# Half-tile products 2 and 4 for a second token group, with their weight sums formed by GpSimd

## The chip, the cores and the metric

One core of one Trainium2 chip runs the whole program. The metric is device time in microseconds (us), taken as the median of several executions; one further execution is recorded by the hardware profiler, and the views below come from it.

## What is computed

Sigmoid attention over 8 batches and 12 heads, then a two-layer network with squared ReLU over the 3584 tokens, all in fp32:

```
scores = q @ k.T / sqrt(64) - log(448)         # 8 x 12 heads, 448 x 448
x = sigmoid(scores) @ v                         # -> 3584 tokens x 768
h = x @ w_in                                    # 768 -> 2048
out = square(maximum(h, 0)) @ w_out             # 2048 -> 768
```

## The kernel before

Every fp32 operand is held as two words, high and low, and every product is three passes of matmuls (high x high, high x low, low x high). The two layers of the network are matrix products in the Strassen-Winograd form: seven products of half-size blocks, numbered 1 to 7, in place of eight. The tokens lie in four groups, g = 0 to 3; each half of a group holds 512 tokens (256 in the last). A group has two stages: the first (`gemm1`, m = 0) multiplies x by w_in, the second (`gemm2`, m = 1) multiplies the squared result by w_out. A step of the first stage is (n, i): product n, block i of the eight blocks of 128 rows of half of the hidden width. It is nine matmuls of 512 columns, three chunks of the depth by three passes.

`STEPS` says in what order a stage's steps come, `sequence` strings the stages together. `run_steps` walks over it and at each step issues what `stream` has put there for later steps: the load of a unit of weights LOAD_AHEAD = 9 steps before its use, and its split into two words HALVE_AHEAD = 5 steps before (ScalarE makes the high word, VectorE the low one; `halve`, L391 and L393). A unit of first-stage weights is up to two products of one block, 128 x 768 numbers: products 1 and 2 together, then 6 and 7, then 3 and 5, and 4 alone. The order of instructions on each engine is then left to a scheduler, except on TensorE in the stage of group `PAIRED`.

In that stage (group 2 before) two blocks are worked on together, and products 2 and 4 have a *halved* form: a second level of the same scheme on the first two chunks of two blocks, seven products of 128 x 256 (`seven`, L440), and the third chunk in the plain form (L678). The halved form needs four sums of 128 x 128 pieces of the weights of each block pair. Before, these are made during group 1's first stage by `prepare`: SyncE (SP) loads the pieces, VectorE adds and splits them, SP stores them; group 2 loads them back (`fetch_sums`).

PSUM has eight banks in four pools of two. `bank` gives the next pool by a counter, `turn`, modulo three, unless a pool is named; the fourth (number 3) is only given by name. After a product that starts or ends a sum, ScalarE copies the bank out (`snap`, L859, or `put`, L1108 with a store by ScalarE at L1109). Before, the first two steps of group 1's first stage are products 1 and 2 of block 0, in banks named ha and hc; oa are the output banks of a second stage.

## Time and profile before

| | us |
|---|---|
| median of 3 runs | 1049.09 (1049.04 to 1049.69) |
| the profiled execution | 1049.4 |
| its span in the trace | 1047.4 |
| group 1, first stage (474.26 to 588.50) | 114.24 |
| group 2, first stage (700.58 to 813.38) | 112.80 |

The span is what the profiler saw, from the first to the last instruction; the rest of an execution lies around it. A stage's length is the distance between the first matmuls of two stages. A row of a timeline gives the start, the duration, the engine, the line, the operation with output and inputs and their shapes, and in brackets for how long the engine was idle before and what ended that.

### The profile page before, as it was taken

How to read it: one execution, taken by the hardware profiler on the slowest of the kernel's cores; microseconds unless marked ns; L12 is line 12 of the kernel's file. 1: busy time of each engine (PE TensorE's matmuls, PEld its weight loads, DVE VectorE, ACT ScalarE, POOL GpSimd, SP SyncE). 2: the span in 40 equal slices, each digit the busy share in tenths (PEclk: the TensorE clock that was granted, in tenths of full speed). 3: DMA queues.
4: the chain of work that ended last, by engine and by line, in shares of the span. 5: the costliest groups of instructions: out<-in, count | busy, mean ns of one | idle time of the engine just before them, and what ended most of it. 6: DMA issues, size and time to landing. Idle time of an engine off the chain costs nothing.

```text
span 1047.4 us, 17472 instructions
## 1 busy us (share of the span) xinstructions
PE 1043.4 (100%) x6490; PEld 820.6 (78%) x6490; DVE 881.1 (84%) x1227; ACT 693.3 (66%) x974; POOL 124.9 (12%) x100
## 2 busy tenths in 40 slices
PE   9999999999999999999999999999999999999998
PEld 4555555557888888888888888888888888899987
DVE  5999999877778899696776799989777999957997
ACT  7989888877667856446444667555435757647973
POOL 1322231200222256300000000110000000000000
PEclk9999999999999999999999999999999999999999
DMA  9999999993567677985574968984445878955662
GB/s 357 400 370 384 343 401 364 329 335 115 185 206 243 213 257 262 335 310 186 169 234 129 320 219 289 323 285 150 139 133 190 273 254 312 316 182 184 182 204 97
DMA packets 127445, 266.45 MB, mean 254 GB/s; under 512 B 12160, under 2 KB 66176, under 8 KB 127360
## 3 DMA queue, kind: packets, MB, share of 16 engines
q1 hardware_dynamic: 125920, 262.91, 73.5%
q10 hardware_dynamic: 1440, 2.43, 0.6%
q8 instruction: 51, 0.84, 0.3%
q14 instruction: 34, 0.28, 0.1%
HBM read 199.75 MB, written 65.54 MB: 253 GB/s over the span
## 4 chain that ended last, share of the span: by engine, by line
PE 100%; DVE 0%; issue 0%
PE ha L678 22%; PE oa L678 19%; PE pav L365 11%; PE sc L334 9%; PE hb L678 8%; PE oq L440 6%; PE ob L678 5%; PE hc L678 3%; PE oc L678 3%; PE oa L686 2%; PE hq L440 2%; PE sr L350 2%; PE pav L377 2%; PE hb L686 1%; PE ob L686 1%; PE oa L689 1%
## 5 line engine op out<-in xcount | busy, mean ns | idle before, releaser
L393 DVE TENSOR_TENSOR w<-w 128x768 fp32r<-128x768 f32 (+1 forms) x159 | 146.7, 931 | 44.0 <-ACT w L391 32.9
L391 ACT CAST w<-w 128x768 fp32r<-128x768 f32 (+1 forms) x160 | 124.2, 795 | 44.9 <-DMA w<-w 42.9
L322 ACT ACTIVATE at<-sc 128x896 f32<-128x896 f32 x144 | 119.3, 943 | 3.9 <-PE sc L334 3.9
L365 PE MATMUL pav<-at,v 64*64 64x448 f32 x1152 | 118.1, 540 | 0.0
L365 PEld LDWEIGHTS pav<-at,v 64*64 64x64 f32 x1152 | 41.6, 133 | 60.8 <-issue 53.6
L786 ACT CAST w<-w 128x768 fp32r<-128x768 f32 x56 | 46.7, 836 | 39.4 <-DMA w<-w 34.5
L859 ACT COPY s<-ha 128x512 f32<-128x512 f32 (+1 forms) x48 | 24.8, 516 | 71.4 <-PE ha L678 65.2
L224 POOL TENSOR_TENSOR a<-a,f 128x768 int32<-128x768 int32 x24 | 52.8, 2202 | 159.5 <-DVE a L221 94.1
L644 DVE TENSOR_TENSOR ql<-x,qh 128x896 fp32r<-128x896 f32 x46 | 67.9, 1518 | 0.0
L334 PE MATMUL sc<-qh 64*128 64x448 f32 x282 | 53.9, 379 | 0.0
L334 PE MATMUL sc<-ql,qh 64*128 64x448 f32 x282 | 51.3, 360 | 0.0
L334 PE MATMUL sc<-qh,ql 64*128 64x448 f32 x282 | 50.9, 358 | 0.0
L387 DVE TENSOR_TENSOR xo<-pav,xo 128x448 f32<-128x448 f32 x48 | 29.5, 621 | 24.4 <-ACT xo L383 22.6
L678 PE MATMUL oa<-o_0h,w 128*128 128x512 f32 x144 | 46.3, 389 | 0.0
L678 PE MATMUL oa<-o_1h,w 128*128 128x512 f32 x144 | 46.3, 389 | 0.0
L678 PE MATMUL oa<-o_2h,w 128*128 128x512 f32 x144 | 46.3, 389 | 0.0
L678 PE MATMUL oa<-o_3h,w 128*128 128x512 f32 x144 | 46.3, 389 | 0.0
L678 PE MATMUL ha<-x_0h,w 128*128 128x512 f32 x128 | 44.7, 390 | 0.0
L678 PE MATMUL ha<-x_2h,w 128*128 128x512 f32 x128 | 44.6, 389 | 0.0
L678 PE MATMUL ha<-x_1h,w 128*128 128x512 f32 x128 | 44.6, 389 | 0.0
L334 PEld LDWEIGHTS sc<-qh 64*128 64x128 f32 x282 | 26.4, 184 | 18.5 <-PE pav L365 16.2
L383 ACT COPY xo<-pav 128x448 f32<-128x448 f32 x48 | 25.5, 532 | 22.6 <-PE pav L377 10.9
(660 smaller groups left out, 3045.7 us busy)
## 6 DMA issues: line engine op xcount, KB each, us to landing
w<-w SPq DMA_DIRECT2D x195, 384.0 KB, 3.7
w<-h SPq DMA_DIRECT2D x56, 384.0 KB, 4.8
x<-qk SPq DMA_DIRECT2D x47, 448.0 KB, 6.8
f<-w_in SPq DMA_DIRECT2D x16, 768.0 KB, 9.0
v<-v SPq DMA_DIRECT2D x24, 448.0 KB, 6.8
xd<-xo SPq DMA_DIRECT2D x48, 224.0 KB, 5.4
h<-w SPq DMA_DIRECT2D x28, 384.0 KB, 4.1
w<-s SPq DMA_DIRECT2D x48, 192.0 KB, 7.5
```

Of the source, the lines that this page charges most:

```text
L224: nc.gpsimd.tensor_tensor(out=wb, in0=wb, in1=t.bitcast(I32)[:, :, 0], op=ALU.add)
L322: nc.scalar.activation(at, sc, AF.Sigmoid, bias=NEG_LOG_S, scale=SCALE)
L334: nc.tensor.matmul(sc[:, j], x[kp][rows, 1, ks], x[qp][rows, 0], start=(n == 0), stop=(n == len(passes) - 1),)
L365: nc.tensor.matmul(sums[columns, h], vt[rows, n % 2 * NT + t, columns], at[t][rows, j], start=(t == 0 and (n % 2, h) != (1, 1)), stop=(t = ...
L387: nc.vector.tensor_add(out=x, in0=sums[:, 0], in1=x)
L391: nc.scalar.copy(out=hi, in_=raw)
L393: nc.vector.tensor_sub(out=lo, in0=raw, in1=hi.bitcast(F32))
L440: nc.tensor.matmul(out, a, b, start=opens and c == 0 and half == 0, stop=closes and c == 2, skip_group_check=True)
L644: nc.vector.tensor_sub(out=xs[n][1], in0=x[n], in1=xs[n][0].bitcast(F32))
L678: nc.tensor.matmul(out, a[:, c], b, start=first and n == 0, stop=last and n == 2, skip_group_check=True)
L686: nc.tensor.matmul(out, w[0][:, c], x, start=first, stop=False, skip_group_check=True)
L786: nc.scalar.copy(out=hi, in_=hi.bitcast(F32))
```

## The change

- `PAIRED` becomes (1, 2): group 1's first stage has the form that group 2's has, products 2 and 4 halved, in the same order of steps, with TensorE's order fixed.
- In groups 1 and 2 a unit of first-stage weights is one product of two blocks (128 x 2 x 384 numbers, runs of 1536 bytes) where it was two products of one block (runs of 3072 bytes).
- `prepare` goes. In group 1 the sums are formed from the unit already loaded: GpSimd adds (`add_sums`, five steps ahead of the use), ScalarE and VectorE split (`split_sums`, three steps ahead), SP stores them for group 2 (`keep_sums`, at the use). Group 2 fetches them as before.
- The differences of x that the halved form needs are made for group 1 too, on GpSimd (`differ`), and group 1's operands of x follow the table `PAIRED_X`.

```
@@ -67,10 +67,8 @@
 LEAD = [(1, 0), (2, 0), (1, 1), (2, 1), (6, 0), (7, 0), (6, 1)]
 LEAD += [(5, 0), (7, 1), (3, 0), (1, 2), (2, 2), (4, 0)]
 
-CROSS = LEAD[:-4] + [(4, 0), (3, 0), (1, 2), (2, 2)]
 STEPS = LEAD + [s for s in ROUNDS if s not in LEAD] + TAIL, ROUNDS + TAIL
-STEPS += (CROSS + [s for s in ROUNDS if s not in LEAD] + TAIL,)
-PAIRED, HALVES_IN = 2, (2, 4)
+PAIRED, HALVES_IN = (1, 2), (2, 4)
 STEPS += ([(n, i + e) for i in range(0, NI, 2) for n in (1, 6, 2, 7, 5, 4, 3) for e in range(2)],)
 
 BEHIND = {512: [(7, Y), (5, Y), (4, Y), (3, Y)], 256: [(7, Z), (4, Y)]}
...
@@ -497,7 +494,7 @@
                 split_to(hi, lo, t, later)
 
         def differ(product, name):
-            if g == PAIRED:
+            if g in PAIRED:
                 raw["d", product] = flat2(f"xd{product}_{g}")
                 flat = raw[name][0].rearrange("p k s -> p (k s)")
                 differences(flat, raw["d", product], lambda **t: nc.gpsimd.tensor_tensor(op=ALU.subtract, **t))
@@ -691,16 +688,14 @@
 
     def order_of(g, m):
         if m == 0:
-            return STEPS[(0, 2, 3, 1)[g]]
+            return STEPS[(0, 2, 2, 1)[g]]
         return ORDERS if g < NG - 1 else [*ORDERS[:-NI], LAST]
 
     sequence = [(g, m, n, i) for g in range(NG) for m in range(2) for n, i in order_of(g, m)]
 
     def units_of(g, m, n, i):
-        if m == 0 and g == PAIRED:
-            if n == 4:
-                return [(g, m, i - i % 2, SPOT[n][0])]
-            return [(g, m, j, SPOT[n][0]) for j in ((i, i + 1) if n == 2 and i % 2 == 0 else (i,))]
+        if m == 0 and g in PAIRED:
+            return [(g, m, i - i % 2, n)]
         if m == 0:
             return [(g, m, i, SPOT[n][0])]
         return [(g, m, j, n) for j in (range(NI // 2) if i < 0 else (i // 2,))]
@@ -715,8 +710,8 @@
     def fetch(unit):
         g, m, i, u = unit
         both = m == 1 and g in TWICE_IN
-        if m == 0 and g == PAIRED and u == SPOT[4][0]:
-            src = w1[i : i + 2, :, UNITS[u].start].rearrange("i p c -> p i c")
+        if m == 0 and g in PAIRED:
+            src = w1[i : i + 2, :, PLACE[0][u]].rearrange("i p c -> p i c")
         elif m == 0:
             src = w1[i][:, UNITS[u]]
         else:
@@ -729,56 +724,58 @@
                     nc.sync.dma_start(out=t.bitcast(F32), in_=s2[i, TWICE.index(u), :, c])
             else:
                 raw_sums[unit] = op1(f"s{m}_{g}_{i}_{u}", WIDE)
-                weight_sums(loaded[unit][1].bitcast(F32), raw_sums[unit])
+                raw = loaded[unit][1].bitcast(F32)
+                weight_sums([raw[:, k, e * P : e * P + P] for e in range(2) for k in range(2)], raw_sums[unit])
 
     summed, raw_sums, front = {}, {}, {}
 
-    def weight_sums(raw, to):
-
-        a11, a12, a21, a22 = (raw[:, k, e * P : e * P + P] for e in range(2) for k in range(2))
+    def weight_sums(parts, to):
+
+        a11, a12, a21, a22 = parts
         s1, s2, s3, s4 = (to[:, n * P : n * P + P] for n in range(4))
         nc.gpsimd.tensor_tensor(out=s1, in0=a21, in1=a22, op=ALU.add)
         nc.gpsimd.tensor_tensor(out=s2, in0=s1, in1=a11, op=ALU.subtract)
         nc.gpsimd.tensor_tensor(out=s3, in0=a11, in1=a21, op=ALU.subtract)
         nc.gpsimd.tensor_tensor(out=s4, in0=a12, in1=s2, op=ALU.subtract)
 
-    halves, half_sums = {}, {}
-
-    def prepare(i, n):
-
-        def load():
-            halves[i, n] = t = flat2(f"sa{n}_{i}")
-            src = w1[i : i + 2, :, PLACE[0][n], : 2 * P].rearrange("i p c -> p i c")
-            nc.sync.dma_start(out=t[:, :WIDE].rearrange("p (i c) -> p i c", i=2), in_=src)
-
-        def add_up():
-            t = halves[i, n]
-            a11, a12, a21, a22 = (t[:, k * P : k * P + P] for k in range(4))
-            s_1, s_2, s_3, s_4 = (t[:, k * P : k * P + P] for k in range(4, 8))
-            nc.vector.tensor_add(out=s_1, in0=a21, in1=a22)
-            nc.vector.tensor_sub(out=s_2, in0=s_1, in1=a11)
-            nc.vector.tensor_sub(out=s_3, in0=a11, in1=a21)
-            nc.vector.tensor_sub(out=s_4, in0=a12, in1=s_2)
-            halves[i, n] = both = flat2(f"sh{n}_{i}", F32R)
-            split_to(both[:, :WIDE], both[:, WIDE:], t[:, WIDE:])
-
-        def store():
-            to = s1[i // 2, HALVES_IN.index(n)]
-            nc.sync.dma_start(out=to, in_=halves.pop((i, n)).bitcast(F32))
-
-        return load, add_up, store
+    half_sums, raw_halves = {}, {}
+
+    def half_sum_tiles(unit):
+        g, m, i, n = unit
+        half_sums[unit] = tuple(op1(f"sf{n}_{g}_{i}{c}", WIDE, F32R) for c in "hl")
+        return half_sums[unit]
+
+    def add_sums(unit):
+        g, m, i, n = unit
+        raw = loaded[unit][1].bitcast(F32)
+        t = raw_halves[unit] = flat2(f"sa{n}_{i}")[:, :WIDE]
+        weight_sums([raw[:, e, k * P : k * P + P] for e in range(2) for k in range(2)], t)
+
+    def split_sums(unit):
+        split_to(*half_sum_tiles(unit), raw_halves.pop(unit))
+
+    def kept_sums(unit):
+        g, m, i, n = unit
+        return s1[i // 2, HALVES_IN.index(n)].rearrange("p (c s) -> c p s", s=WIDE)
+
+    def keep_sums(unit):
+        for to, t in zip(kept_sums(unit), half_sums[unit]):
+            nc.sync.dma_start(out=to, in_=t.bitcast(F32))
 
     def fetch_sums(unit):
-        i, n = unit
-        half_sums[unit] = tuple(op1(f"sf{n}_{i}{c}", WIDE, F32R) for c in "hl")
-        for c, t in enumerate(half_sums[unit]):
-            src = s1[i // 2, HALVES_IN.index(n)][:, c * WIDE : c * WIDE + WIDE]
+        for t, src in zip(half_sum_tiles(unit), kept_sums(unit)):
             nc.sync.dma_start(out=t.bitcast(F32), in_=src)
 
-    for i in range(0, NI, 2):
-        for n in HALVES_IN:
-            use = sequence.index((PAIRED, 0, n, i))
-            stream.setdefault(use - HALF_SUMS_AHEAD[n], []).append((fetch_sums, (i, n)))
+    for unit in units:
+        g, m, i, n = unit
+        if m == 0 and g in PAIRED and n in HALVES_IN:
+            use = first_use[unit]
+            if g == PAIRED[0]:
+                pieces_at = (HALVE_AHEAD, add_sums), (SUMS_SPLIT, split_sums), (-SUMS_KEPT, keep_sums)
+            else:
+                pieces_at = ((HALF_SUMS_AHEAD[n], fetch_sums),)
+            for ahead, piece in pieces_at:
+                stream.setdefault(use - ahead, []).append((piece, unit))
 
     def halve(unit, later=None):
         if unit[1] == 1 and unit[0] in TWICE_IN:
...
@@ -865,16 +862,16 @@
                 nc.vector.tensor_add(out=t, in0=both[:, n_tok:], in1=t)
 
         def weights_at(n, i):
+            if g in PAIRED:
+                return tuple(t[:, i % 2] for t in loaded[g, 0, i - i % 2, n])
             u, at = SPOT[n]
-            if n == 4:
-                i, at = i - i % 2, i % 2
             return tuple(t[:, at] for t in loaded[g, 0, i, u])
 
         def halved(n, i):
 
             for at in range(4):
                 banks["q", at] = bank(f"hq{n}_{g}_{i}_{at}", WIDE, 2 + at // 2)
-            w, s = [weights_at(n, i + e) for e in range(2)], half_sums.pop((i, n))
+            w, s = [weights_at(n, i + e) for e in range(2)], half_sums[g, 0, i, n]
 
             def part(k, h):
                 return tuple(t[:, h * Q : h * Q + Q] for t in ops[n][k])
...
@@ -926,17 +923,16 @@
         def run(n, i):
             count = len(pending)
             k = CHAIN[n]
-            if g == PAIRED and n in HALVES_IN:
+            if g in PAIRED and n in HALVES_IN:
                 run_halves(n, i)
                 return
-            if g == PAIRED and n in (1, 7):
+            if g in PAIRED and n in (1, 7):
                 banks[k, i] = bank(f"h{k}_{g}_{i}", n_tok, (1, 7).index(n))
             elif n in (1, 7, 2):
                 banks[k, i] = bank(f"h{k}_{g}_{i}", WIDE if n in BESIDE else n_tok, 3 if k == "c" else None)
             out = banks[k, i]
             beside = n_tok < WIDE and n in BESIDE
-            u, at = SPOT[n]
-            w = tuple(t[:, at].rearrange("p (c m) -> p c m", m=P) for t in loaded[g, 0, i, u])
+            w = tuple(t.rearrange("p (c m) -> p c m", m=P) for t in weights_at(n, i))
             parts = [(out, w, c, ops[n][c], n in (1, 7, 2) and c == 0, c == NE - 1) for c in range(NE)]
             if beside:
                 side_by_side(parts)
@@ -975,7 +971,7 @@
             run(n, i)
             if (n, i) in behind:
                 operand(behind[n, i])
-            if g == PAIRED and (n, i) == STEPS[3][-1]:
+            if g in PAIRED and (n, i) == STEPS[2][-1]:
                 while next(turn) % 3 < 2:
                     pass
 
@@ -1210,7 +1206,7 @@
                 for name in LATE_X.get((n, i), ()) if g == NG - 2 else ():
                     next_x[g][name]()
             if m == 0 and 0 < g < NG - 1:
-                for name in (PAIRED_X if g == PAIRED else EARLY_X).get(at - sequence.index((g, 0, *order_of(g, 0)[0])), ()):
+                for name in PAIRED_X.get(at - sequence.index((g, 0, *order_of(g, 0)[0])), ()):
                     next_x[g - 1][name]()
 
     made, second, next_x, postponed, now = {}, {}, {}, {}, [0]
@@ -1265,17 +1261,14 @@
         for n, piece in work:
             between.setdefault(n, []).append(piece)
         run_steps(0, len(STEPS[0]), between)
-    between = {}
-    begin = sequence.index((PAIRED - 1, 0, *order_of(PAIRED - 1, 0)[0])) + PREPARE_FROM
-    for n, (i, k) in enumerate((i, k) for i in range(0, NI, 2) for k in HALVES_IN):
-        load_piece, add_piece, store_piece = prepare(i, k)
-        for ahead, piece in ((0, load_piece), (4, add_piece), (6, store_piece)):
-            between.setdefault(begin + n * PREPARE_EVERY + ahead, []).append(piece)
-    first, second_stage = (sequence.index((PAIRED, m, *order_of(PAIRED, m)[0])) for m in range(2))
-    run_steps(len(STEPS[0]), first, between)
-    with tc.manual_schedule(engines={mybir.EngineType.PE}):
-        run_steps(first, second_stage, between)
-    run_steps(second_stage, len(sequence), between)
+    begin = len(STEPS[0])
+    for g in PAIRED:
+        first, second_stage = (sequence.index((g, m, *order_of(g, m)[0])) for m in range(2))
+        run_steps(begin, first, {})
+        with tc.manual_schedule(engines={mybir.EngineType.PE}):
+            run_steps(first, second_stage, {})
+        begin = second_stage
+    run_steps(begin, len(sequence), {})
 
 
 def kernel(q, k, v, moe_w_in, moe_w_out):
```

What moves on the engines is shown at three places. The first is TensorE at the start of group 1's first stage, with the semaphores that a row waits for; ha_1_0 and ha_1_1 are the banks of product 1, blocks 0 and 1, of group 1. Before:

```order
L678 MATMUL ha_1_0_5282<-y1_1l_5038,w0_1_0_0_5178 128x512
L678 MATMUL ha_1_0_5282<-y1_1h_5037,w0_1_0_0_5178 128x512
L678 MATMUL hc_1_0_5304<-x2_1h_5076,w0_1_0_0_5178 128x512
L678 MATMUL hc_1_0_5304<-x2_1l_5077,w0_1_0_0_5178 128x512
L678 MATMUL hc_1_0_5304<-x2_1h_5076,w0_1_0_0_5178 128x512 x2
```

And there TensorE has now:

```order
L675 MATMUL ha_1_0_5294<-y1_1l_5038,w0_1_0_1_5183 128x512
L675 MATMUL ha_1_0_5294<-y1_1h_5037,w0_1_0_1_5183 128x512
L675 MATMUL ha_1_1_5310<-x1_1h_5035,w0_1_0_1_5183 128x512 [waits Activation_49]
L675 MATMUL ha_1_1_5310<-x1_1l_5036,w0_1_0_1_5183 128x512
L675 MATMUL ha_1_1_5310<-x1_1h_5035,w0_1_0_1_5183 128x512 x2
```

Product 2 of block 0, in the fourth pool, stood second; now product 1 of block 1 does, and its first matmul waits for ScalarE, for the copy of the bank's last content, oa_0_2.

The second place is ScalarE there: w0_... are units of weights, o12_0_0 to o12_0_2 the copies of group 0's last output blocks, sf2_1_0h the high words of the first set of sums. Before:

```order
L391 CAST w0_1_0_1_5226<-w0_1_0_1_5226 128x768
L1108 COPY o12_0_0_5260<-oa_0_0_4289 128x512
L1109 DMA outT<-o12_0_0_5260 128x512
L1108 COPY o12_0_1_5274<-oa_0_1_4290 128x512
L1109 DMA outT<-o12_0_1_5274 128x512
L1108 COPY o12_0_2_5277<-oa_0_2_4291 128x512
L1109 DMA outT<-o12_0_2_5277 128x512
L859 COPY s1_1_0_5292<-ha_1_0_5282 128x512
L391 CAST y7_1h_5298<-yx11_1_4939 128x512
```

And ScalarE now:

```order
L388 CAST w0_1_0_2_5231<-w0_1_0_2_5231 128x768
L1104 COPY o12_0_0_5265<-oa_0_0_4289 128x512
L1105 DMA outT<-o12_0_0_5265 128x512
L1104 COPY o12_0_1_5277<-oa_0_1_4290 128x512
L1105 DMA outT<-o12_0_1_5277 128x512
L1104 COPY o12_0_2_5280<-oa_0_2_4291 128x512
L388 CAST sf2_1_0h_5321<-sa2_0_5283 128x512
L1105 DMA outT<-o12_0_2_5280 128x512
L388 CAST y7_1h_5331<-yx11_1_4939 128x512
L856 COPY g11_1_0_5304<-ha_1_0_5294 128x512
```

The copies keep their order behind the cast of a weight unit; the cast of the sums and that of y7 now stand ahead of the copy of product 1, block 0.

The third place is GpSimd from the last sums of group 0's second stage on: xd2_1 and xd4_1 are differences of x of group 1, sa2_0 and sa4_0 the sums for products 2 and 4 of the first block pair. Before:

```order
L743 TENSOR_TENSOR s1_0_3_4_4959<-w1_0_3_4_4957,s1_0_3_4_4959 128x128
L503 TENSOR_TENSOR xd2_2_7113<-x21_2_6946 128x256 x2
L503 TENSOR_TENSOR xd2_2_7113<-x21_2_6946,xd2_2_7113 128x256 x2
L503 TENSOR_TENSOR xd4_2_7379<-x21_2_6946 128x256 x2
L503 TENSOR_TENSOR xd4_2_7379<-x21_2_6946,xd4_2_7379 128x256 x2
```

And GpSimd now:

```order
L739 TENSOR_TENSOR s1_0_3_4_4959<-w1_0_3_4_4957,s1_0_3_4_4959 128x128
L500 TENSOR_TENSOR xd2_1_5097<-x21_1_4942 128x256 x2
L500 TENSOR_TENSOR xd2_1_5097<-x21_1_4942,xd2_1_5097 128x256 x2
L736 TENSOR_TENSOR sa2_0_5283<-w0_1_0_2_5231 128x128
L738 TENSOR_TENSOR sa2_0_5283<-w0_1_0_2_5231 128x128
L737 TENSOR_TENSOR sa2_0_5283<-sa2_0_5283,w0_1_0_2_5231 128x128
L739 TENSOR_TENSOR sa2_0_5283<-w0_1_0_2_5231,sa2_0_5283 128x128
L500 TENSOR_TENSOR xd4_1_5350<-x21_1_4942 128x256 x2
```

Where GpSimd had nothing between group 0's second stage and group 2's operands, it now makes the differences of group 1 and eight sets of four sums.

## Rows read from the trace of the kernel before

**Rows 1.** The page: busy time with shares and instructions; shares of the ending chain.
```profile
PE 1043.4 (100%) x6490; PEld 820.6 (78%) x6490; DVE 881.1 (84%) x1227; ACT 693.3 (66%) x974; POOL 124.9 (12%) x100
...
PE 100%; DVE 0%; issue 0%
```

**Rows 2.** Table by stretches, one stage each: length, busy time by engine, clock, DMA.
```profile
core 0: us, PE busy (x) PEld busy (x) DVE busy (x) ACT busy (x) POOL busy (x), PEclk, DMA share, GB/s
364.14:474.26 110.12, 110.12 (x488) 91.18 (x486) 98.38 (x101) 62.20 (x81) 43.25 (x48) 1.00 0.86 296
474.26:588.50 114.24, 114.24 (x506) 94.59 (x504) 78.09 (x119) 55.98 (x88) 0.00 (x0) 1.00 0.59 191
588.50:700.58 112.08, 112.08 (x614) 97.78 (x612) 104.36 (x145) 70.20 (x87) 6.50 (x6) 1.00 0.83 283
700.58:813.38 112.80, 112.80 (x578) 96.71 (x576) 89.73 (x123) 57.60 (x86) 1.64 (x3) 1.00 0.51 162
```

**Rows 3.** TensorE's timeline: first matmuls of steps in group 1, then group 2.
```profile
474.26 0.39 PE L678 MATMUL ha<-x_1h,w 128*128 128x512 f32 x1
...
476.30 0.39 PE L678 MATMUL hc<-x_1h,w 128*128 128x512 f32 x1
...
708.74 0.28 PE L440 MATMUL hq<-x_2h,w 128*128 128x256 f32 x1
...
712.64 0.39 PE L678 MATMUL hb<-x_2h,w 128*128 128x512 f32 x1
```

**Rows 4.** ScalarE's timeline just ahead of group 2's first stage.
```profile
698.06 0.59 ACT L1108 COPY o<-oa 128x512 f32<-128x512 f32 x1 [5.32 <-PE oa L678]
```

**Rows 5.** ScalarE's timeline at the start of group 1's first stage; ACTq is its queue.
```profile
473.67 0.84 ACT L391 CAST w<-w 128x768 fp32r<-128x768 f32 x1 [1.32 <-DMA w<-w]
474.40 0.58 ACT L1108 COPY o<-oa 128x512 f32<-128x512 f32 x1
475.02 2.74 ACTq L1109 DMA_DIRECT2D outT<-o  x1
477.80 0.59 ACT L1108 COPY o<-oa 128x512 f32<-128x512 f32 x1 [2.81 <-issue]
...
478.82 0.59 ACT L1108 COPY o<-oa 128x512 f32<-128x512 f32 x1 [0.44 <-PE hc L678]
...
479.87 0.59 ACT L859 COPY s<-ha 128x512 f32<-128x512 f32 x1 [0.47 <-ACT o L1108]
480.35 0.62 ACT L391 CAST y_1h<-yx 128x512 fp32r<-128x512 f32 x1
```

**Rows 6.** L1109 alone, ScalarE's stores: duration ns least/median/most, first and last start.
```profile
L1109 ACTq DMA_DIRECT2D outT<-o x9: 338/339/2737, 475.0 to 926.3; - x9
```

**Rows 7.** GpSimd's groups by line and shape: sums of weights (busy, mean ns, idle before).
```profile
L742 POOL TENSOR_TENSOR s<-w 128x128 f32<-128x128 f32 x12 | 12.5, 1042 | 0.0
L741 POOL TENSOR_TENSOR s<-s,w 128x128 f32<-128x128 f32 x12 | 12.3, 1023 | 0.1
L740 POOL TENSOR_TENSOR s<-w 128x128 f32<-128x128 f32 x12 | 10.7, 896 | 48.6 <-DMA w<-w 48.6
L743 POOL TENSOR_TENSOR s<-w,s 128x128 f32<-128x128 f32 x12 | 9.0, 750 | 0.5
```

**Rows 8.** VectorE's groups by line and shape: low words of `prepare`'s sums.
```profile
L393 DVE TENSOR_TENSOR sh<-sa,sh 128x512 fp32r<-128x512 f32 x8 | 5.5, 686 | 0.8 <-ACT sh L391 0.7
```

**Rows 9.** VectorE's timeline: one operation beside GpSimd's sums, one without.
```profile
373.18 1.20 DVE L393 TENSOR_TENSOR w<-w 128x768 fp32r<-128x768 f32 x1 [0.90 <-POOL s L743]
...
472.41 0.95 DVE L393 TENSOR_TENSOR w<-w 128x768 fp32r<-128x768 f32 x1
```

**Rows 10.** L296, landing of weight loads: 364 to 460 us, then 479 to 560.
```profile
DMA to landing us min/median/max: 3.2/4.3/8.5
...
DMA to landing us min/median/max: 2.3/3.3/4.6
```

**Rows 11.** SP's timeline ahead of group 1's first stage: its third unit.
```profile
468.73 0.37 SPq L296 DMA_DIRECT2D w<-w  x1
```

11 lines of the change are left out of this document (5 added, 6 removed).

## The prediction

> **What bounds the kernel now.** I read the shares of busy time and the chain of work first. TensorE is busy for 1043.4 of 1047.4 us and the chain that ended last is 100% TensorE [rows 1], so the time changes only by what TensorE has to do and by the pauses that it gets. Then the table by stretches, one row a stage. Group 1's first stage, the one that the change rewrites, is 474.26 to 588.50: 114.24 us, TensorE busy for all of it. Group 2's, 700.58 to 813.38, already has the form that group 1 is to get: 112.80 us, TensorE again never idle [rows 2]. The other engines have room in both: VectorE 78.09 and 89.73 us, ScalarE 55.98 and 57.60, GpSimd 0 and 1.64, and the granted clock is 1.00, the 2.4 GHz level [rows 2]. Last, TensorE's and ScalarE's timelines where the stage begins, since that is where the instructions move most.
>
> The profiled execution took 1049.4 us: its span of 1047.4 and 2.0 around it. The median of the runs is 1049.1, that is 0.3 less. I add up against 1049.4 and take the 0.3 off at the end.
>
> **What the change can give.** A step of nine 512-column matmuls takes 476.30 - 474.26 = 2.04 us, a pair of steps 4.08. In group 2 a halved pair goes from 708.74 to 712.64: 3.90 us [rows 3]. Each halved pair saves 0.18; products 2 and 4 have four pairs each, so 8 x 0.18 = 1.44 us. The stages say the same: 114.24 - 112.80 = 1.44 [rows 2]. **Term 1: -1.44 us.** As TensorE never idles in the stage today there is nothing else to win: 1.44 us, 0.14% of the time, is the ceiling. A measurement of this kernel can tell about 0.2% (2.1 us) from no change, so a full success would read as no change. What decides is whether TensorE now pauses somewhere.
>
> **The pause that the order adds.** Group 0's last product, 3, leaves three output blocks oa in three PSUM banks. ScalarE copies them out (L1108) and issues a store after each (L1109). In the order of before the second step of group 1's stage is product 2, whose bank hc is of the fourth pool and waits for nothing. In the order of after the second step is product 1, block 1, and its first matmul waits for ScalarE. The bank it is given is that of oa_0_2, the *third* copy: the paired form fixes product 1 to pool 0, and group 0's stages leave the counter `turn` where oa's blocks 0, 1, 2 lie in pools 1, 2, 0. Group 2 has the same step and does not suffer, since after a paired stage the counter is set so that block 0 lies in pool 0: only the first copy stands ahead of it, at 698.06, almost 2 us before the stage begins [rows 4, 2].
>
> ScalarE at that place in before: the cast of a weight unit at 473.67, the first copy at 474.40, a store whose issue takes 2.74 us, the second copy at 477.80, the third at 478.82 for 0.59, so to 479.41 [rows 5]. That store is the first of nine that ScalarE issues; the median of the nine is 0.339 us and the largest 2.737 [rows 6]. The order of after has the same sequence (weight cast, copy, store, copy, store, copy) and again this is the first transfer that ScalarE issues, so I take the long issue to come back, in the same place. TensorE reaches the step at 476.30 [rows 3] and the bank is free at 479.41: **term 2: 479.41 - 476.30 = +3.11 us.** Bounds: without the long issue the copies follow 1.02 us apart (478.82 - 477.80), the third from 474.40 + 2 x 1.02 = 476.44 to 477.03, and the wait is 0.73. Below nothing it cannot go, since TensorE waits for nothing at this place today. The row at this very place has the long issue; I take 3.11.
>
> What TensorE does next is product 6, block 0, into the bank of product 1, block 0, which must have been copied. Behind the third copy ScalarE now has the cast of the new sums, a store, a cast of y7 and that copy: 479.41 + 0.62 + 0.34 + 0.62 + 0.59 = 481.58 by [rows 5, 6], and casts overlap by some 0.1 there. TensorE ends product 1 at 479.41 + 2.04 = 481.45. **Term 3: 0** (bounds 0 and +0.2; when the third copy is early, up to +0.5, since the cast waits for GpSimd's sums).
>
> **The sums on GpSimd.** A set of four 128x128 operations takes 0.896 + 1.042 + 1.023 + 0.750 = 3.71 us [rows 7], eight sets 29.7 us, in a stage of 113 where GpSimd has nothing else but the eight operations for the differences. A set is begun five steps (10 us) ahead of its use and split after two. It hides behind TensorE; if a set came late, the halved product would wait for it. VectorE loses the adds of the sums and keeps their second words: 8 x 0.686 = 5.5 us [rows 8], on group 2's 89.73: 95.2. Beside GpSimd one VectorE operation on 128x768 took 1.20 us where it takes 0.95 alone [rows 9]; a quarter us for some 32 operations is 8 us, an estimate, and makes 103 of 112.8. Group 1's second stage runs at 104.36 of 112.08 without a pause, and in group 0's second stage GpSimd made such sums (43.25 us) beside 98.38 us of VectorE, TensorE still busy for all of 110.12 [rows 2]. **Term 4: 0**, up to +1 if a late set meets a bank.
>
> This is where a rule speaks against the change. In [rows 9] GpSimd lengthens an operation of VectorE by 0.25 us. The Trainium skill, page "SBUF — State Buffer", section "Who interferes with whom", says that GpSimd has no ports of its own but VectorE's second pair, and that this pair is an exclusive lock. By the rows the stage costs VectorE 103 us and nothing of the time; by the rule taken in full, 125 us, the rival below.
>
> **Weight loads.** The units of groups 1 and 2 become one product of two blocks: as many bytes, in runs of 1536 bytes where they were 3072. The second stages read such runs: loads landed in 3.2, 4.3 and 8.5 us (least, median, most) in group 0's second stage; in group 1's first stage with the long runs in 2.3, 3.3 and 4.6 [rows 10]. The DMA share is 0.86 in the one stretch and 0.59 in the other [rows 2], so the runs are not the whole difference. Loads are asked for nine steps, 18 us, ahead; 8.5 is covered, **term 5: 0**. The one place with less cover is the start of the stage, where the third unit was asked for at 468.73 and its cast began at 473.67, 4.94 us later [rows 11, 5]. That cast stands ahead of the three copies on ScalarE, in both orders. **Other edits** at no price: the early loads and VectorE adds of `prepare` go (2 MB less to read), the stores of the sums move to the steps that use them, behind operands long made; the operands of x come by the table that group 2 has, where they were in time.
>
> **Sum.** -1.44 + 3.11 + 0 + 0 + 0 = +1.67: 1049.4 + 1.67 = 1051.07 for the profiled run, less 0.3: **1050.8 us**.
>
> **The rivals.**
> *Short issue.* The store's issue takes 0.34 us, or the copies come before it. Wait 0.73, then up to 0.5 for the copy of product 1: -1.44 + 1.23 = -0.2, 1048.9. For it: eight of nine issues are short, and nothing that the long one waited for was open. Against: the long one is the first, and the first stays the first.
> *The gain in full.* The scheduler's order runs so that the copies are out by 476.3: 1047.65. Against: TensorE's last matmul into oa_0_2 ends about where the stage begins, and three copies with two stores are over 2 us of ScalarE.
> *A later landing (slower).* The third unit is now product 2 of two blocks, 256 short runs. If it lands later than the 4.94 us of before, its cast holds the three copies and the bank one for one. 8.5 us, the longest landing [rows 10], would add 3.6; I take +1.5, so 1052.3. It decides from a delay of 0.4 us. For it: the DMA engines are busiest there. Against: the median, 4.3, is below 4.94.
> *The clock falls.* TensorE has not paused at any place of before, and the granted clock was 1.00 in every row [rows 2]. If a pause of 3 us drops it to the 1.2 GHz level, each step of 2.04 us takes 4.08 until it rises; one to two steps cost 2 to 4, I take 3: 1053.8. The Trainium skill, page "TensorE: Matmul & The Clock Gate", section "HAM oscillation — how this bites in real kernels", tells of a clock lost in waits between bursts of matmuls; no row of this trace shows it.
> *VectorE becomes the bound.* If every us of GpSimd stops VectorE, the stage takes 95.2 + 29.7 = 124.9 us where it took 114.24: 10.7 more, 1059.8. Against: group 0's second stage, where 98.38 + 43.25 fitted into 110.12 [rows 2]. The rule on the ports named above would have it so.
> That the change does not do what it says is ruled out by the order: the halved steps and the sums stand where they should.
>
> **How the numbers follow.** Forecast 0.49 (own range 1050.2 to 1051.4); short issue 0.24; gain in full 0.05; later landing 0.13; clock 0.07; VectorE 0.02. "Within 0.2%" is 1047.0 to 1051.2. Slower: a fifth of the forecast's case lies above 1051.2 (0.10), with landing, clock and VectorE 0.32. Faster: only an error in term 1 gets below 1047.0, 0.01. The rest, 0.67, is the same. The range 1048.2 to 1052.6 leaves out the full gain, the clock, VectorE and the upper end of a late landing: 0.18.
>
> **What would show it.** In the trace of after: a gap on TensorE at the second step of group 1's first stage, about 3.1 us, ended by ScalarE's copy, and a first store on ScalarE of 2.7 us ahead of it; apart from the gap 112.8 us for the stage; no other gap; the clock at 1.00; GpSimd at some 38 us in the stage (29.7 and the 8.1 that the differences took in group 2, 6.50 + 1.64 in [rows 2]), VectorE at 95 to 103. No gap or one of 0.7 with a short first store makes term 2 wrong; a gap in each halved step would make terms 4 or 5 wrong; a stage not shorter by 1.4 without its gaps makes term 1 wrong.

## The result, and the profile after

The changed kernel took 1055.28 us (median of 6 runs; five lie between 1054.43 and 1055.76, the sixth took 5317.66 and is not in the ratio) against 1049.17 before: a ratio of 1.0058, 95% interval 1.0044 to 1.0072, so 6.1 us slower. The forecast was 1050.8, its range ended at 1052.6. The profiled execution, the fastest of these, took 1054.43, its span is 1052.6, 5.2 more than before.

The page's shares of busy time and its chain of work, which were [rows 1]:

```profile
PE 1044.0 (99%) x6562; PEld 823.6 (78%) x6562; DVE 905.4 (86%) x1241; ACT 699.5 (66%) x980; POOL 154.8 (15%) x140
...
PE 87%; DVE 4%; POOL 3%; DMA 3%; issue 2%; SPq 1%; ACTq 0%; ACT 0%; DVEq 0%; POOLq 0%
```

The chain is no longer all TensorE: it runs through DMA, VectorE, GpSimd and SP. TensorE has less to do by 1.44 us and yet is busy for 0.6 longer, so it ran at a lower clock somewhere. The table by stretches (length, busy time of TensorE, its weight loads, VectorE, ScalarE, GpSimd, granted clock, DMA share, GB/s), with group 1's two stages, group 2's first one, and then the start of group 1's first stage in two pieces, against [rows 2]:

```profile
474.06:593.22 119.16, 114.71 (x578) 97.62 (x576) 98.54 (x131) 63.39 (x98) 24.16 (x36) 0.99 0.54 170
593.22:705.66 112.44, 112.40 (x613) 97.71 (x612) 107.01 (x149) 68.59 (x83) 6.71 (x7) 1.00 0.82 278
705.66:818.46 112.80, 112.80 (x577) 96.71 (x576) 91.27 (x124) 58.28 (x87) 1.39 (x2) 1.00 0.54 171
...
474.06:480.71 6.65, 2.20 (x11) 1.51 (x9) 1.79 (x2) 2.55 (x5) 6.05 (x11) 0.97 0.82 304
480.71:484.25 3.54, 3.54 (x9) 2.85 (x10) 2.58 (x3) 3.00 (x5) 1.42 (x3) 0.58 0.73 272
```

The loss sits at the start of group 1's first stage: 119.16 us where the form itself takes 112.80 (group 2, unchanged). The first step, with the pause behind it, is 6.65 long instead of 2.04: 4.61, of which the row below shows 4.45 as idle, counted from the end of the last matmul. The second step, 480.71 to 484.25, is 3.54 long instead of 2.04 at a granted clock of 0.58: 1.50. The rest of the stage makes 0.25. The next stage is 0.36 longer (112.44 against 112.08), which was not traced to a cause. With the saving: -1.44 + 4.61 + 1.50 + 0.25 + 0.36 = +5.28; the stage begins 0.20 earlier and some 0.1 is added later, which is the 5.2 of the span.

TensorE's and ScalarE's timelines at that place (start, duration, engine, line, operation; in brackets the idle time before and what ended it):

```profile
480.71 0.79 PE L675 MATMUL ha<-x_1h,w 128*128 128x512 f32 x1 [4.45 <-ACT o L1104]
484.25 0.39 PE L675 MATMUL ha<-x_1h,w 128*128 128x512 f32 x1
```

```profile
474.46 0.84 ACT L388 CAST w<-w 128x768 fp32r<-128x768 f32 x1 [1.07 <-DMA w<-w]
475.21 0.58 ACT L1104 COPY o<-oa 128x512 f32<-128x512 f32 x1
475.82 3.10 ACTq L1105 DMA_DIRECT2D outT<-o  x1
479.02 0.58 ACT L1104 COPY o<-oa 128x512 f32<-128x512 f32 x1 [3.23 <-issue]
...
480.07 0.58 ACT L1104 COPY o<-oa 128x512 f32<-128x512 f32 x1 [0.47 <-ACT o L1104]
...
481.67 0.58 ACT L856 COPY g<-ha 128x512 f32<-128x512 f32 x1
```

TensorE waits at product 1, block 1, for the third copy, as forecast. But measured from the start of the stage the third weight unit is split at +0.40, where it was at -0.59 in [rows 5]: 0.99 later. The first store takes 3.10 us, not 2.74, and from the first copy to the third it is 4.86 instead of 4.42. SP had asked for the unit at 469.33, 4.73 ahead of the start, where [rows 11] has 5.53: the later request is 0.80 of the 0.99, and from the request to the split it is 5.13 instead of 4.94, the other 0.19. So the third copy ends at +6.59 instead of +5.15: 1.44 later, and the wait that I put at 3.11 is 4.55 by the same sum, where 4.45 and 4.61 were measured.

### The profile page after: what moved, and what is told of

Same layout as the page of the kernel before. It is cut to its first block, busy times and chain, and to the rows that moved or that the text cites. A ratio compares the mean times of both kernels' runs of the same rounds, so it can differ in the third digit from the quotient of the medians.

```text
span 1052.6 us, 17721 instructions
## 1 busy us (share of the span) xinstructions
PE 1044.0 (99%) x6562; PEld 823.6 (78%) x6562; DVE 905.4 (86%) x1241; ACT 699.5 (66%) x980; POOL 154.8 (15%) x140
## 4 chain that ended last, share of the span: by engine, by line
PE 87%; DVE 4%; POOL 3%; DMA 3%; issue 2%; SPq 1%; ACTq 0%; ACT 0%; DVEq 0%; POOLq 0%
PE ha L675 21%; PE oa L675 13%; PE pav L362 11%; PE sc L331 9%; PE hb L675 7%; PE oq L437 6%; PE hq L437 4%; PE ob L675 2%; DMA w<-w 2%; PE oa L683 2%; PE sr L347 2%; PE pav L374 2%; PE hc L675 2%; PE ob L683 1%; PE hb L683 1%
## 5 line engine op out<-in xcount | busy, mean ns | idle before, releaser
L955 ACT ACTIVATE g<-ha 128x512 f32<-128x512 f32 (+1 forms) x32 | 17.3, 544 | 38.8 <-PE ha L675 38.8
L856 ACT COPY s<-hb 128x512 f32<-128x512 f32 x32 | 18.8, 587 | 34.8 <-PE hb L675 32.0
```

## The experiments

Theory A is that the whole loss is one chain: a weight unit lands late, its split stands ahead of the copies on ScalarE, a long store stands between them, the bank waits for the third; the clock falls behind the pause. The rivals are that the bank alone is to blame, that the two-block units land slowly by themselves, and that GpSimd or VectorE costs TensorE time in the stage. The cuts of code are against the changed kernel, and the ratio is to the kernel before, measured beside each run.

| run | median us | ratio to before, 95% |
|---|---|---|
| bank_first_copy | 1054.02 | 1.0045 (1.0031 to 1.0059) |
| early_first_store | 1052.02 | 1.0028 (1.0018 to 1.0037) |
| late_third_cast | 1054.81 | 1.0051 (1.0037 to 1.0066) |
| no_scalar_chain | 1051.0 | 1.0021 (1.0011 to 1.003) |
| stores21_scalar | 1051.51 | 1.0024 (1.0015 to 1.0033) |
| no_stores21 | 1051.84 | 1.0026 (1.0016 to 1.0036) |
| vector_sums_only | 1055.16 | 1.0057 (1.0043 to 1.0071) |
| split_later | 1051.63 | 1.0023 (1.0013 to 1.0032) |
| vector_sums_no_chain | 1050.63 | 1.0014 (1.0005 to 1.0022) |
| gathered | 1052.72 | 1.003 (1.0019 to 1.0042) |
| gathered_vector | 1052.27 | 1.0029 (1.0018 to 1.0041) |
| gathered_light | 1048.17 | 0.9987 (0.9978 to 0.9996) |
| gathered_pool | 1053.03 | 1.0034 (1.0022 to 1.0047) |
| gathered_early_words | 1049.23 | 1.0002 (0.9993 to 1.0011) |
| gathered_early_vector | 1049.44 | 1.0004 (0.9995 to 1.0013) |

### The bank

```
-banks[k, i] = bank(..., (1, 7).index(n))          +banks[k, i] = bank(..., (1, 7).index(n) + 1)
-banks["q", at] = bank(..., 2 + at // 2)           +banks["q", at] = bank(..., at // 2 * 3)
-while next(turn) % 3 < 2:                         +while next(turn) % 3 != 0:
```

> Edit: products 1 and 7 and the halved products of groups 1 and 2 take their PSUM pools one further round, so that product 1, block 1, gets the bank of group 0's first output block instead of the third; nothing else moves. Theory A (a chain on ScalarE: weight cast, copy, long first store, copy, store, copy): the pause of 4.45 us at the second step goes, but the third step, product 6, waits for ScalarE's copy of product 1, block 0, which stands behind all three copies and ended at 482.25 in the changed kernel, where TensorE would now be ready at 478.1: a pause of about 4.1 us one step later, the clock falls as before, 1054 to 1055 us. Rival B (the bank alone is the cause): no pause, 1048 to 1049.5 us.

TensorE's waits in the stage:

```profile
476.25 0.50 PE L675 MATMUL ha<-x_1h,w 128*128 128x512 f32 x1 [0.19 <-ACT o L1104]
482.59 0.50 PE L675 MATMUL ha<-x_1h,w 128*128 128x512 f32 x1 [4.01 <-ACT g L856]
```

The pause moves one step on and keeps its size, 4.01 us, now behind the copy of product 1, block 0, which stands behind the same three copies. The stage is 119.44 long. Theory A holds; the bank is where the chain ends, not what makes it long.

### The first store of ScalarE

```
-(nc.scalar if add is None else nc.sync)
+(nc.scalar if add is None or (g, name, e) == (0, "11", 0) else nc.sync)
```

> Edit: one store of group 0's product 2, some 60 us earlier, is issued by ScalarE instead of SP, so that the store after the first copy is no longer ScalarE's first. Theory A1 (the long issue belongs to the first store of ScalarE): the early store takes about 3 us, the one after the first copy 0.34, the third copy ends at about 477.9, the pause is 1.8 us instead of 4.45; 1050.3 us if the clock then stays at 1.00, 1051.8 if it falls. Rival A2 (the long issue belongs to the place, where loads crowd the queues): the store there again takes about 3 us, the pause stays at 4.4, about 1054.5 us.

ScalarE's timeline, at the early store and at the copies, and TensorE's wait:

```profile
395.12 0.38 ACTq L1105 DMA_DIRECT2D outT<-o  x1
...
475.69 0.83 ACT L388 CAST w<-w 128x768 fp32r<-128x768 f32 x1 [1.34 <-DMA w<-w]
476.43 0.58 ACT L1104 COPY o<-oa 128x512 f32<-128x512 f32 x1
477.04 0.34 ACTq L1105 DMA_DIRECT2D outT<-o  x1
```

```profile
479.16 0.50 PE L675 MATMUL ha<-x_1h,w 128*128 128x512 f32 x1 [3.12 <-ACT o L1104]
```

The store between the copies is short now, 0.34 us, and the pause shorter, though not 1.8 us: here the weight unit was split at 475.69, 1.23 later than in the changed kernel. Neither explanation of the long issue holds alone: the early store, ScalarE's first, took 0.38 us, so being first does not make it long, and the place does not either. It was long only where both came together; why stays open. The pause of 3.12 was followed by a fall of the clock.

### The split of the third unit

```
-... (halve at) use - HALVE_AHEAD            +... + 2 * (unit == (1, 0, 0, 2))
```

> Edit: the split of group 1's third weight unit (product 2, used four steps into the stage) is asked for two steps later, so that it no longer stands ahead of the three copies on ScalarE. Theory A: the copies start about 1.9 us earlier (473.3 instead of 475.21), the long store comes with them, the third copy ends near 478.8, the pause is 2.7 us instead of 4.45; 1052.7 us with the clock falling, 1051.2 without. Rival C (the landing of the two-block unit matters in itself, by the loads or the sums that follow): the pause stays above 4 us or a second one comes at the halved product, 1054 to 1056 us.

```profile
480.02 0.50 PE L675 MATMUL ha<-x_1h,w 128*128 128x512 f32 x1 [3.35 <-ACT o L1104]
501.81 0.39 PE L437 MATMUL hq<-xd_1h,sf_0l 128*128 128x256 f32 x1 [1.12 <-DVE sf_0l L390]
```

The first copy began at 474.14 instead of 475.21, since the *second* unit now held it (its split began at 473.40), the store took 3.49 us, and the pause shrank by 1.1 only. A second wait of 1.12 appeared, for VectorE, at the halved product 4, and the stage stayed as long (119.42). Neither expectation names both; the time, 1054.81, lies in the range of rival C, though the second wait is for VectorE and not for the load.

### Why the unit lands late

Loads stand behind stores on SP that wait for VectorE, and by the rows VectorE is late through the change itself. VectorE and GpSimd in group 0's second stage, in the kernel before (GpSimd ends its last sum at 444.45) and in the changed kernel:

```profile
444.48 0.96 DVE L393 TENSOR_TENSOR w<-w 128x768 fp32r<-128x768 f32 x1 [3.58 <-POOL s L743]
445.36 1.22 DVE L393 TENSOR_TENSOR x_1l<-x,x_1h 128x1024 fp32r<-128x1024 f32 x1
446.50 1.22 DVE L393 TENSOR_TENSOR o_1l<-g,o_1h 128x1024 fp32r<-128x1024 f32 x1
```

```profile
443.43 1.48 DVE L390 TENSOR_TENSOR w<-w 128x768 fp32r<-128x768 f32 x1 [2.37 <-POOL s L739]
444.83 1.76 DVE L390 TENSOR_TENSOR x_1l<-x,x_1h 128x1024 fp32r<-128x1024 f32 x1
446.51 1.76 DVE L390 TENSOR_TENSOR o_1l<-g,o_1h 128x1024 fp32r<-128x1024 f32 x1
...
445.47 3.40 POOL L500 TENSOR_TENSOR xd<-x,xd 128x256 f32<-128x256 f32 x2
```

From 443.35 to 448.87 GpSimd now makes group 1's first differences. Three operations of VectorE beside them take 1.60 us more in all; VectorE began them 1.05 earlier and ends them 0.56 later. It has no gap from there to 468, and SP's request for the third unit comes 0.60 later. No run took the differences away from there, so this is read from rows and not tested.

The first of two runs lets ScalarE issue those stores, the second leaves them out.

```
stores21_scalar:  +(nc.scalar if add is None or (g, name) == (0, "21") else nc.sync)
no_stores21:      +if (g, name) != (0, "21"):   (store)
```

> Edit: the changed kernel, with the three stores of group 0's product 4 issued by ScalarE instead of SP, nothing else. They wait for VectorE's additions, and in the trace of the changed kernel the loads of group 1's second and third weight units stand behind them on SP. Theory A (the pause is a chain: VectorE late, SP's stores late, third unit late, its cast late, copies late, and in it ScalarE's long first store): the third unit is asked for near 466.7 instead of 469.33, lands by 472, ScalarE's long issue falls at about 465 where nothing waits for it, the third copy ends near 475: no pause at product 1, clock 1.00; 1047.7 us if nothing is next, 1049 to 1050.3 if the halved products then wait 1 to 2.5 us for VectorE, as they did without the chain. Rival C (the landing of the two-block units is itself slow): the pause stays above 3 us, 1052 to 1055.

> Edit: the changed kernel without the three stores of group 0's product 4 (that third of group 0's output is left out, so the time is read without 0.79 MB of writes). In the run where ScalarE issued these stores the third weight unit was asked for 3 us earlier (466.31) and its cast still waited until 474.38, with the DMA engines busy in full from 464 to 480. Theory F (the third unit lands when the bytes ahead of it have gone through, some 400 GB/s): 0.79 MB less are 2 us, the cast begins at about 472.5, the third copy ends 2 us earlier, the pause is 2.0 to 3.0 us instead of 4.45; 1051 to 1052.5 us. Rival C (the two-block unit with its short runs takes 8 us to land by itself): its cast stays at 474 or later, pause above 4 us, 1054 to 1055.

In stores21_scalar, SP's issue of the third unit, its split on ScalarE, and the table of three stretches ahead of the stage (the last three columns are clock, DMA share, GB/s):

```profile
466.31 0.37 SPq L293 DMA_DIRECT2D w<-w  x1
```

```profile
474.38 0.83 ACT L388 CAST w<-w 128x768 fp32r<-128x768 f32 x1 [3.05 <-DMA w<-w]
```

```profile
464.00:468.00 4.00, 4.00 (x20) 3.30 (x19) 4.00 (x7) 1.61 (x2) 0.00 (x0) 1.00 1.04 402
468.00:472.00 4.00, 4.00 (x19) 3.34 (x18) 4.00 (x5) 0.91 (x2) 0.00 (x0) 1.00 1.05 402
472.00:476.00 4.00, 3.86 (x18) 2.85 (x16) 0.92 (x2) 1.32 (x2) 1.49 (x4) 1.00 1.04 394
```

Asked for 3 us earlier (466.31 against 469.33), the unit landed at the same time, 8.0 us after the request: the DMA engines were full throughout, at 394 to 402 GB/s. The pause was 1.88 us for another reason, the store between the copies took 0.34; waits of 0.45 and 0.71 for VectorE came behind it. So neither expectation held: theory A had no pause, rival C one above 3. Without the stores' bytes:

```profile
473.16 0.84 ACT L388 CAST w<-w 128x768 fp32r<-128x768 f32 x1 [0.99 <-PE oa L675]
...
474.51 2.82 ACTq L1106 DMA_DIRECT2D outT<-o  x1
```

```profile
479.08 0.50 PE L675 MATMUL ha<-x_1h,w 128*128 128x512 f32 x1 [2.54 <-ACT o L1104]
```

The split began at 473.16, 1.3 us earlier than in the changed kernel, the pause was 2.54 with the long store still there, and the clock stayed at 1.00 in this execution. The split still waited for the load, whatever its bracket names: the unit was asked for at 465.49 and took 7.6 us to land, and GpSimd's first sum from it began at 473.19, at the same moment. So in these two runs the unit lands when the bytes ahead of it have gone through. The short runs add nothing where the DMA engines are less busy: from 479 to 560 the changed kernel's loads landed in these times (least, median, most), with the same median as the long runs of before [rows 10]; at the start of the stage no run tells them apart.

```profile
DMA to landing us min/median/max: 3.1/3.3/4.2
```

### GpSimd

```
-nc.gpsimd.tensor_tensor(...)   +engine.tensor_tensor(...)     (engine = nc.vector for group 1)
```

> Edit: the changed kernel with group 1's weight sums on VectorE instead of GpSimd, nothing else. Theory A: the pause at product 1 does not depend on who forms the sums, since the third copy stands ahead of them on ScalarE: pause 4.3 to 4.7 us, clock as before, 1054.5 to 1055.5. Rival D (GpSimd beside VectorE costs TensorE time in the stage): 1.5 us or more less, 1053.5 or below.

The pause was 3.92 us, the stage 118.71, the time 1055.16, the same as the changed kernel's. Who forms the sums does not matter for the time while the chain is there.

### The chain taken out

Bank, SP for the three last stores, the third unit's split two steps later, and the sums' split behind the copy before it:

```
+(nc.scalar if add is None and g > 0 else nc.sync)
 def split_sums(unit):
+    with tc.issue_after(front["act"].ins):
         split_to(...)
```

> Edit: bank of the first copy, group 0's last stores issued by SP instead of ScalarE, the third unit's split two steps later, and the split of the sums not ahead of the copy of the product before it. Theory A: no pause in group 1's first stage and the clock at 1.00, the stage 112.8 to 113.1 us; against the changed kernel 4.6 (pause) and 1.5 (clock) less: 1048.0 to 1048.5 us, about 0.1% faster than the kernel before. Rival D (GpSimd's sums, the short-run loads or the stores of the sums cost TensorE time of their own): stage of 114 us or more, or pauses at the halved steps, 1050 us or more.

```profile
483.07 0.38 PE L437 MATMUL hq<-x_1h,w 128*128 128x256 f32 x1 [0.57 <-DVE w L390]
497.11 0.38 PE L437 MATMUL hq<-xd_1l,sf_0h 128*128 128x256 f32 x1 [1.48 <-DVE xd_1l L390]
497.71 0.39 PE L437 MATMUL hq<-xd_1h,sf_0l 128*128 128x256 f32 x1 [0.22 <-DVE sf_0l L390]
```

No wait for ScalarE is left and the clock is 1.00, but the stage takes 115.94: at the halved products of the first block pair TensorE now waits for VectorE's low words. Theory A was right on the pause and wrong on what lies behind it; 3.1 us over 112.80 remain, 2.27 of them in these three waits, the rest not traced.

### What is next: VectorE

Two runs change the order of the sums' split and then also who forms the sums:

```
split_later:           (SUMS_SPLIT - 2 * (unit == (1, 0, 0, 2)), split_sums), no hold
vector_sums_no_chain:  the same, with the sums on nc.vector
```

> Edit: as the run without the chain on ScalarE (bank of the first copy, group 0's last stores by SP, third unit's split two steps later), but the split of the first sums is only asked for two steps later instead of being held behind the copy before it. Theory A2 (what remained there, 1.5 + 0.6 + 0.2 us, was VectorE's order at the start of the stage, filled badly by the hold): VectorE works through y7 and y5 while TensorE is in the first step, so the halved products wait less than 1 us in all: 1048 to 1049.3. Rival E (VectorE has too much to do in the first 20 us of the stage, in any order): again 2 us or more of pauses at the halved products, 1050 to 1051.

> Edit: as the run before, with the sums of the weights in group 1 formed by VectorE instead of GpSimd. In the run without the chain VectorE's operations beside GpSimd's sums took 0.3 to 0.5 us longer (1.58 instead of 1.22 us), some 1.8 us up to the first halved product; on VectorE a set takes four short operations, some 0.8 to 1.2 us in all. If the slowing by GpSimd is what makes VectorE late: pauses at the halved products shrink by about 1 us, 0.5 to 1 us less than the run before. If VectorE is simply full: 1 us more than the run before.

In split_later the pauses were 0.42 and 0.63 us at product 6, behind ScalarE's copies of product 1's two blocks, and 0.77 and 0.40 behind VectorE, the stage 116.57. In vector_sums_no_chain they were 0.97 behind such a copy and 0.22 behind VectorE, the stage 114.92. Neither order fills it well; without GpSimd's sums the median was 1.0 us lower, though the two intervals overlap.

The next two gather what helped: bank, early store, the splits of the second and third unit later, and the sums held behind product 1's first copy only; in the second run with the sums on VectorE.

```
+more = {(1, 0, 0, 6): 2, (1, 0, 0, 2): 2}.get(unit, 0)
+(SUMS_SPLIT + (unit == (1, 0, 0, 2)), split_sums)
```

> Edit: the changed kernel with the bank of the first copy, one earlier store by ScalarE (so that the long first issue lies where nothing waits), the splits of the second and third unit two steps later, and the first sums' split held behind the copy of product 1, block 0, alone. Theory A2: the chain at the start is gone (copies done by 477, product 1's copy by 477.5), what is left are waits for VectorE at the halved products of the first block pair, 0.5 to 1.5 us: 1048.3 to 1049.5 us. Rival E (VectorE is full in the first 20 us): 2 us or more of pauses, 1050 to 1051.

> Edit: as the run before, with group 1's weight sums on VectorE instead of GpSimd. Theory A2 with GpSimd's slowing of VectorE as part of the rest: 0.5 to 1 us less than the run before, 1047.8 to 1048.8 us, the first to lie below the kernel before. Rival E: the same as the run before or more.

```profile
483.54 0.39 PE L437 MATMUL hq<-x_1h,w 128*128 128x256 f32 x1 [0.27 <-DVE w L390]
497.10 0.39 PE L437 MATMUL hq<-x_1h,w 128*128 128x256 f32 x1 [1.24 <-DVE w L390]
498.83 0.39 PE L437 MATMUL hq<-xd_1h,sf_0l 128*128 128x256 f32 x1 [1.12 <-DVE sf_0l L390]
```

In the profiled execution of gathered every wait for ScalarE is gone, and 2.63 us behind VectorE are there instead. It is not the typical one: its clock was 1.00, while five of the other six had 0.998, as runs whose clock fell have. VectorE on the sums made it no better here: 0.85, 0.22, 0.61 and 1.50 us of waits, stage 117.10. The rival E holds for the waits, and the times, 1052.72 and 1052.27, lie above its range. The table shows the first 26 us of the stage, of the kernel before (group 1, then group 2) and of gathered; VectorE's is the third busy time in a row:

```profile
474.26:500.26 26.00, 26.00 (x116) 21.55 (x115) 15.47 (x19) 16.04 (x27) 0.00 (x0) 1.00 0.50 157
700.58:726.58 26.00, 26.00 (x136) 22.37 (x135) 22.07 (x28) 17.86 (x26) 1.64 (x3) 1.00 0.52 161
```

```profile
474.42:500.42 26.00, 23.37 (x118) 19.33 (x117) 22.37 (x25) 20.27 (x32) 13.47 (x16) 1.00 0.65 226
```

VectorE had 15.47 us of work there before, now 22.37, with a gap of 3.15 us at 475.6 in which it waits for ScalarE. Group 2 has 22.07 and no wait, so the sum alone does not decide. Taking work away tests it:

```
+if g == 1 and product in (3, 4, 5, 7):       # gathered_light: the high word in the low word's place
+    ops[product] = [(hi, hi) for hi, _ in ops[product]]
```

> Edit: as the gathered version, but group 1's operands of x for products 7, 5, 4 and 3 get no low word (the high word is used in its place, so that group 1's numbers are coarser), which takes eight operations, some 7.5 us, from VectorE in the first 30 us of the stage; TensorE's work is the same. Rival E, now the theory (behind the chain on ScalarE stands VectorE, with 22 to 24 us of work in the first 26 us of the stage where the kernel before had 15.5): the pauses at the halved products, 2.6 us in all in the gathered version, go to below 0.5, the stage is 112.8 to 113.3 us, and the whole 1.44 us is there: 1047.5 to 1048.3 us. Rival G (the waits are not VectorE's amount of work but late loads or late sums): pauses of 2 us or more stay, 1050 or more.

```profile
474.02:586.82 112.80, 112.80 (x577) 96.72 (x576) 92.55 (x122) 63.50 (x97) 27.85 (x36) 1.00 0.56 180
```

The stage takes 112.80 us, as group 2's, TensorE never idle: the gain of term 1 nearly in full, 1048.17 us against 1049.48 for the kernel before. The kernel leaves those low words out and is no version to use. Rival G, late loads, does not explain it: its loads lay some 1.0 us earlier against the stage's start than in gathered's profiled execution, but no_scalar_chain had them within 0.2 us of these (the second unit's split 1.58 ahead of the start, here 1.76; the first sum 0.37 behind it, here 0.29) and kept its waits.

### Can it be had with all of the work

```
gathered_pool:         nc.gpsimd makes the low words of xd2 and xd4 of group 1, xd2's in group 0's second stage
gathered_early_words:  next_x[0][7]() at step (3, 5) of group 0's second stage; squares("11", 1) of group 1 on ScalarE
gathered_early_vector: the same, with the sums on nc.vector
```

> Edit: as the gathered version, with the two low words of group 1's differences made by GpSimd instead of VectorE, the first of them already in group 0's second stage, where GpSimd and ScalarE have idle time. It takes 2.4 us of work from VectorE in the first 26 us of the stage and leaves nothing out. Theory E: pauses at the halved products 1 us or less instead of 2.6, 1048.0 to 1049.5 us. If GpSimd's slowing of VectorE eats it: as the gathered version, 1050 to 1052.

GpSimd's and VectorE's timelines in gathered_pool at the second of these low words, and TensorE's wait at the first:

```profile
491.66 3.42 POOL L506 TENSOR_TENSOR xd_1l<-xd,xd_1h 128x1024 fp32r<-128x1024 f32 x1 [4.18 <-ACT xd_1h L505]
...
492.74 3.42 DVE L912 TENSOR_TENSOR g<-g,he 128x1024 f32<-128x1024 f32 x1
...
472.81 0.73 PE L679 MATMUL oa<-o_3h,w 128*128 128x512 f32 x2 [1.79 <-DVE w L390]
```

An operation that takes VectorE 1.22 us took 3.42 beside GpSimd's, and ended 1.08 after it. GpSimd's first low word, 5.46 us long from 462.95, did the same to a VectorE operation of 0.68 us, which took 2.29 and ended 0.55 after it; the four operations of VectorE that began before that one kept their usual times. Behind this TensorE paused for 1.79 us already in group 0's second stage, and 1.26 us after it resumed its clock fell:

```profile
474.07:477.72 3.65, 3.65 (x10) 2.83 (x9) 2.25 (x3) 1.58 (x3) 0.00 (x0) 0.53 1.03 391
```

The stage then began at 478.19, 3.8 us later than in gathered, and took 115.01, 1.6 less. Moving work to GpSimd moved the loss and did not shrink it (1053.03 against 1052.72).

> Edit: as the gathered version, with two pieces of VectorE's work moved out of the first 26 us of group 1's first stage and nothing left out: product 7's operand of x is split near the end of group 0's second stage, where ScalarE waits some 4 us for a weight unit and VectorE has gaps, and the squaring after the first halved pair goes to ScalarE. That is 3.1 us less on VectorE there. Theory E (VectorE's amount and order of work is what is left): the pauses at the halved products fall from 2.6 us to less than 1, 1047.9 to 1049.0 us, below the kernel before. Otherwise, when the moved split delays the weight units ahead of the stage: pauses of 2 us or more, 1050 or more.

> Edit: as the run before, with group 1's weight sums on VectorE instead of GpSimd. If GpSimd's slowing of VectorE (1.2 us operations taking 1.5) outweighs the sums' own time on VectorE (0.28 us an operation): 0.3 to 0.8 us less than the run before; if not, the same or up to 0.8 more.

```profile
473.83:586.88 113.05, 113.05 (x577) 96.67 (x576) 97.57 (x128) 63.90 (x97) 28.34 (x36) 1.00 0.56 181
```

In the profiled execution of gathered_early_words TensorE has no pause in the stage, and that execution took 1048.13 us. VectorE is busy for 22.97 of its first 26 us, more than in gathered: so that sum does not decide; as far as the edit shows, what counts is which operations stand ahead of those that the halved products wait for, and here product 7's were done before the stage began. But the median of its runs is 1049.23 (1048.13 to 1051.11): what the longer executions met is not recorded. The start of the stage hangs on loads, and in the five versions that split the third unit ahead of the copies and keep all bytes the split came between 474.38 and 475.69. The version recovers the loss, and the gain does not show: the run is not told apart from the kernel before. With the sums on VectorE it is the same, 1049.44.

## Why the prediction was wrong

- **Term 1** (-1.44) is right: 112.80 us without pauses, and 1.3 us faster in gathered_light.
- **Term 2** (+3.11) had place, mechanism and releaser right; the size is 4.61. The step that failed is "The row at this very place has the long issue; I take 3.11". That row rested on the landing of a load in one execution of another kernel. The third unit came 0.99 later against the stage's start, and the long store and the copies took 0.44 more. SP asked for the unit 0.80 later against the start, behind stores that waited for VectorE, which by the rows at 443 was itself late beside GpSimd's new differences; the prediction gave these no price ahead of the stage. An earlier request alone does not mend it: in stores21_scalar the DMA engines were full and the unit landed when it had before.
- **The rivals were taken as exclusive.** A later landing (0.13, price 1.5) and a fall of the clock (0.07, price 3) both came, on top of the forecast, since a later landing makes the pause longer. The sum held the clock at nothing. With 1.44 more for the wait and 1.50 for the clock the prediction's own sum gives 1053.7; no line of it added them. What is left to 1055.3 are some 0.4 us in the stages and the median, which lies 0.85 above the profiled execution here where it lay 0.3 below before; the other four executions were granted 0.996 to 0.997 of the clock where the profiled one had 0.998, so they lost more to it than the trace shows. My range ended at the upper part of one rival alone.
- **The clock**: behind pauses of 3.12 to 4.45 us (five kernels) the matmuls that follow ran at about half speed for some 3.5 us: the granted clock was 0.56 to 0.64 in such a stretch, most of it at the 1.2 GHz level (0.50 from 482 to 484 in vector_sums_only), and 1.00 before the pause. It cost 1.50 in the changed kernel, half of the price that I had set without a row for how long it lasts, because the clock came back before the second step ended. That the clock falls behind a wait agrees with the Trainium skill, page "TensorE: Matmul & The Clock Gate", section "HAM oscillation — how this bites in real kernels", which has a clock that is lost when TensorE waits for data between its bursts. The length of the pause does not decide by itself: behind 1.79 us in gathered_pool it fell, behind 1.88 in stores21_scalar and 2.54 in no_stores21 it stayed at 1.00. What else decides is not shown.
- **Term 3** (0) is right: product 6 began at 484.25 without a wait. The copy that it needs ended at 482.25, and at full clock TensorE would have come at 480.71 + 2.04 = 482.75.
- **Term 4** (0) is right for the changed kernel and wrong as an argument. I set 103 us against a stage of 112.8 and compared with other whole stages. What counts, by the last runs, is what VectorE has to finish ahead of the first halved products: it was busy for 15.47 of the stage's first 26 us before, and for 22 to 24 in the versions that do all of the work without the long pause, which hid this in the changed kernel (19.16); with the pause gone 2 to 3 us came back there. A set of sums took 1.8 us where VectorE was idle and up to 4.9 beside it; my 3.71 lies between, and GpSimd was busy for 24.16 us in the stage, not 38. The term left out what GpSimd's differences do to VectorE ahead of the stage.
- **The rule on the ports**: I gave it 0.02 because group 0's second stage held 98.38 + 43.25 us in 110.12. In full it did not come (98.54 us of VectorE in a stage of 119.16, GpSimd 24.16). In single operations VectorE took 3.42 us in place of 1.22 in gathered_pool, ending 1.08 after GpSimd's. This agrees with the exclusive lock of the Trainium skill, page "SBUF — State Buffer", section "Who interferes with whom".
- **Term 5** (0) is right on the short runs away from the start of the stage: from 479 to 560 loads landed in 3.3 us (median), as before. The place with less cover that it named is where the loss began.

## What to carry to other kernels

Where a change fixes the order of the engine that bounds the kernel, look at the first steps of the stage and follow the bank, the copy, the work ahead of that copy, and the load that this waits for, each with the spread of its own time; and add up what can go wrong together, since a later load makes a longer pause and a pause can cost the clock. Busy shares of a stage say little on its first fifth, and the share of that fifth does not settle it either (22.07 and 22.97 us without a wait, 22.37 with one): look at which operations a step waits for, and what stands ahead of them. Here a gain of 0.14% showed only with every wait out, and each wait removed uncovered the next.
